# Strided masks of two batches on VectorE, fewer warm-up products, and expert weights loaded later and from ScalarE

## The chip, the core and the metric

The kernel runs on one core of one Trainium2 chip. The metric is the device time of one execution in microseconds (us). TensorE is written PE in profiles, VectorE DVE, ScalarE ACT, GpSimd POOL, and SyncE SP.

## What is computed

An attention block of 8 batches, 8 heads, 576 tokens and head size 64 is followed by a mixture of 8 experts. Heads 0 to 3 see the last 32 tokens; heads 4 to 7 see the earlier tokens of their own residue class modulo 32.

```python
mask_local = (rel >= 0) & (rel < stride)
mask_strided = (rel >= 0) & (pos[None, :] % stride == pos[:, None] % stride)
scores = np.where(masks[None, :, :, :], scores, -1000000000.0)
attn = softmax(scores);  x = attn @ v
...
e = fresh_e if s == 0 or local_gate[b, s] < 0.5 else prev_e
h = np.maximum(x[b, s] @ w1[e], 0.0)
out[b, s] = p[e] * (h @ w2[e])
```

Each token goes through one expert: the one its own logits choose, or the one of the token before it, as a gate says.

## The kernel before

**Attention.** `attention` walks over 32 head pairs, four to a batch: pairs 0 and 1 are local, 2 and 3 strided. One iteration n issues the load of pair n + 4 (`load`, L169 for q and k, L173 for values), the scores of pair n in two units (`scores`), the transposes of pair n - 2 (`turn_x`, L330), and the values and the normalization of pair n - 1 (`values` L288, `norm` L301 and L302). Router work, logits (L354) and gates (L382) come in fixed iterations, and two lists, `also` and `steps`, hang further work on them. There are five q/k buffers, two score banks in PSUM and two value banks, so a load waits until the scores of the pair five before it are done.

A local unit's mask is a multiplication by 0 and 1 on VectorE after the exponential (`mask`, L275). A strided unit's mask is a product ahead of its scores: an identity times `maskS`, with large negative numbers at the hidden places (L258), into the same bank, onto which the score products (L264) add. `maskS` is built at the start from two index tables.

At the very start `busy(WARM)` issues ten products of zeros (L184), 512 columns each. Products by twos are how f32 shows in the records.

**SyncE's order.** All q, k and value loads are issued by SyncE in the order of the program, and so are the stores of attention's rows to DRAM from batch 1 on (`store_x`): two DMAs for a local half (L314), ten for a strided half (L320). Expert 0's weights come in eight pieces of 512 KB (L724 for w1, L727 for w2), one an iteration from n = 5 to 12, after the load of that iteration. From n = 10, two of the sixteen weight sums of expert 0 (`sums`, L732) run on VectorE at each iteration's end.

**Experts.** `Experts.run` multiplies pairs of row tiles (128 rows each) by an expert's weights with seven products for eight (Strassen-like; `pair_hidden` L835, `pair_output` L871), which needs the sums and differences of weight blocks that `sums` makes. Two weight buffers `W` alternate: while expert e runs, the weights of e + 1 are loaded and summed. For each expert the first pair of tiles runs, then a second (`rest`), and then a `tc.Switch` of seven arms takes the remaining tiles: more pairs, a single tile (L926, L937) or half a tile (L947, L967). `pair_hidden` and `pair_output` call `run(steps)` at nine places, four and five; the lists of lists that `slots` builds say how many pending steps run at each place. Rows are gathered (L765) and scattered (L791) by GpSimd.

The weights of experts 1 to 7 are two SyncE DMAs of 2 MB each, issued as soon as their buffer is free; SyncE is no part of the switch, so it may issue while an arm still runs.

Of the kernel before, what the change touches and what calls it, by code (L numbers as in the profile page):

```python
# [8 lines left out]
F32 = mybir.dt.float32  # L9
# [3 lines left out]
Alu = mybir.AluOpType  # L13
# [5 lines left out]
P = 128  # L19
B, H, S, DH = 8, 8, 576, 64  # L20
# [19 lines left out]
GK, GL = PL * GC, PL * GR  # L40
# [15 lines left out]

TRUST = 1e12

WARM = 10

FILL = 4

TWINS = {b: b - 1 for b in range(1, B - 1, 2) if b % RB}

# [83 lines left out]
def attention(ctx, tc, qkl, qks, vl, vs, wg, xd, ident, router, moe):  # L148

    nc = tc.nc  # L150
    sums, probs, codes = router.sums, router.probs, router.codes
    consts = ctx.enter_context(tc.tile_pool(name="consts", bufs=1))
# [32 lines left out]

    busy(WARM)

# [21 lines left out]
    maskS = consts.tile([GK, 2 * GK + GL], BF16, name="maskS")  # L209
# [3 lines left out]
    for n, c in blocks:  # L213

        i, div = consts.tile([GK, 1], I32, name=f"row{n}"), consts.tile([GK, 1], F32, name=f"div{n}")
# [7 lines left out]
    n = GK  # L223
    nc.vector.tensor_copy(maskS[:, 0:2 * n].rearrange("p (a x) -> p a x", a=2), across(apart[n], [n, 2, n]))
    nc.vector.tensor_copy(maskS[:, 2 * n:], apart[GL])
    fold = consts.tile([P, 32], F32, name="fold")
    ci = consts.tile([P, E], I32, name="ci")
    down = consts.tile([P, E], F32, name="down")
    pi = consts.tile([P, CH], I32, name="pi")
    pos8 = consts.tile([P, CH], F32, name="pos8")  # L230
    start = consts.tile([P, CH], F32, name="start")

    def more_constants():

# [15 lines left out]
    def scores(u):  # L250
        t = st["qk", u.b, u.pair]
        kb, width = (LK, LQ) if u.local else (GK, GK)
        ps = psS.tile([P, 2, 512], F32, name="sps")
        sp = spans(u)
        n = sp[-1][2] + sp[-1][1]
        if not u.local:
            for h in range(2):
                nc.tensor.matmul(ps[0:GK, h, 0:n], lhsT=identb[0:GK, 0:GK],  # L258
                                 rhs=maskS[:, 0:n], start=True, stop=False, skip_group_check=True)
        for j, w, c in sp:  # L260
            m = kb if u.local else w
            for h in range(2):
                r = slice(h * DH, (h + 1) * DH)
                nc.tensor.matmul(ps[0:m, h, c:c + w], lhsT=t[r, S + j * width:S + j * width + m],  # L264
                                 rhs=t[r, j * width:j * width + w],
                                 start=(u.local and c == 0), stop=True, skip_group_check=True)
        e = work.tile([P, 2, 2 * GK + GL], F32, name="e")
        nc.scalar.activation(e[0:kb, :, 0:n], ps[0:kb, :, 0:n], Act.Exp, bias=0.0, scale=1.0 / DH ** 0.5)  # L268
        u.e = e

    def mask(u):
        if u.local:
            ev = u.e[:, :, 0:3 * LQ]
            m = maskL[:, 3 * u.g:3 * u.g + 3].rearrange("p a x -> p (a x)")
            nc.vector.tensor_tensor(ev, ev, m.rearrange("p (o x) -> p o x", o=1).to_broadcast([LK, 2, 3 * LQ]),  # L275
                                    op=Alu.mult)

    def values(u):
# [151 lines left out]
        u.n = n  # L430

    also = {n: [] for n in range(len(units) + 3)}
    also[1] = [more_constants]
    also[2] = [router.constants]
    n = PAIRS * RB + 3
# [4 lines left out]
    m = n  # L440
    rooms = (moe.spot[0].rearrange("p a x -> p (a x)")[:, 0:1024], moe.spot[1].rearrange("p a k x -> p (a k x)"),
             moe.spot[2].rearrange("p i a x -> p (i a x)"))
    early = router.table(0, bank, rooms)
# [5 lines left out]
    steps = []  # L449
    for n in range(len(units) + 3):  # L450
        if n < len(units):
            if n + ahead < len(order):
                load(*order[n + ahead])
            if 5 <= n < 13:
                moe.W[0].load(nc, moe.w1, moe.w2, 0, n - 5)
            if n == 10:
                steps = moe.W[0].sums(nc.vector)
            for u in units[n]:
                scores(u)
                mask(u)  # L460
        if 0 <= n - 2 < len(units) and order[n - 2][1] % 2 == 1:
            store_x(units[n - 2][1])
        if 0 <= n - 2 < len(units) and n != len(units):
            turn_x(*order[n - 2])
        if 0 <= n - 1 < len(units):
            for u in units[n - 1]:
                values(u)
                norm(u)
        if n == len(units):
            turn_x(*order[n - 2])  # L470
            moe.turn(moe.first, spare, 0)
        elif n == len(units) + 1:
            busy(FILL)
        for b in range(B):
            last = PAIRS * b + PAIRS - 1
            if n == last + 3 and b + 1 not in TWINS:
                gates(b)
            if n == last + 4 and b < B - 1 and b + 1 not in TWINS:
                for both in {TWINS.get(b, b), b}:
                    store_p(both)  # L480
            if n == last + 2:
                logits(b)
        for do in steps[:2]:
            do()
            steps.remove(do)
        if n == len(units) + 1:
            moe.turn(moe.first, bank, 1)
            busy(2)
            moe.row_sums(moe.first)
        for do in also[n]:  # L490
            do()
# [215 lines left out]
class Weights:  # L707
# [11 lines left out]
    def load(self, nc, w1, w2, e, piece=None):  # L719

        w1, w2 = w1[e].rearrange("(k p) f -> p k f", p=P), w2[e].rearrange("(k p) f -> p k f", p=P)
        if piece is None or piece < DK:
            c = slice(0, DK) if piece is None else slice(piece, piece + 1)
            nc.sync.dma_start(out=self.w1[:, c], in_=w1[:, c])  # L724
        if piece is None or piece >= DK:
            c = slice(0, FK) if piece is None else slice(2 * (piece - DK), 2 * (piece - DK) + 2)
            nc.sync.dma_start(out=self.w2[:, c], in_=w2[:, c])  # L727

    def sums(self, engine):

# [25 lines left out]
class Experts:  # L756
# [40 lines left out]
    def run(self, ctx):  # L797
        nc, tc, w1, w2, router = self.nc, self.tc, self.w1, self.w2, self.router
# [3 lines left out]
        W = self.W  # L802
# [176 lines left out]
        def load(e, w):  # L979
            w.load(nc, w1, w2, e)  # L980
            return w.sums(nc.vector)

        def slots(todo, counts):

            return [[todo.pop(0) for _ in range(min(n, len(todo)))] for n in counts]
# [13 lines left out]
        def rest(e, w, spot, pair, steps, nxt, index=None):  # L999

            self.gather(nxt)
            if index is None:
                steps = [[lambda: chosen.append(choose(e))]] + steps
            part1, part2 = pair_output(pair, w, pair_hidden(pair, w, steps))
            part1(steps)
            index = index or chosen.pop()
            flip = state["flip"]

            for arm in tc.Switch(index, ARMS, hint=f"expert{e}"):
                state["flip"] = flip  # L1010
                left = list(steps)
                more = []
                if arm > 3:
                    more.append(rows(spot, e, (4, 5)))
                if arm % 4 > 1:
                    more.append(rows(spot, e, (4 + arm // 4 * 2,)))
                if arm % 2:
                    more.append(rows(spot, e, (4 + arm // 2,), HALF))
                if more:
                    self.gather(more[0])  # L1020
                part2(more[0] if more else nxt, left)
                for i, r in enumerate(more):
                    then = more[i + 1] if i + 1 < len(more) else nxt
                    if i + 1 < len(more):
                        self.gather(then)
                    if r.m < P:
                        half(r, w, then, left)
                    elif r.n == 1:
                        single(r, w, then, left)
                    else:  # L1030
                        output(r, w, pair_hidden(r, w, left), then, left)
                while left:
                    run(left)
# [4 lines left out]
        sums = load(1, W[1])  # L1038
# [11 lines left out]
        second = rows(0, 1, (2, 3))  # L1050
# [6 lines left out]
        h = pair_hidden(other, W[1], places)  # L1057
# [1 line left out]
        nxt = rows(1, 0, (2, 3))  # L1059
        rest(1, W[1], 0, second, [[lambda: next(arms)] for _ in range(4)], nxt)  # L1060
        second = nxt
        sums = load(2, W[1])
        nxt = rows(0, 2, (0, 1))
        rest(0, W[0], 1, second, slots(sums, [0, 1, 2, 1, 2, 2, 2, 2]) + [[f] for f in sums], nxt)
        for e in range(2, E - 1):
            w, first = W[(e + 1) % 2], nxt
            second = rows(1, e, (2, 3))
            self.gather(second)
            steps = slots(load(e + 1, W[e % 2]), [0] * 5 + [1, 1, 1, 3] + [1] * 8 + [2])
            nxt = rows(0, e + 1, (0, 1))  # L1070
            h = pair_hidden(first, w, steps)
            index = choose(e)
            output(first, w, h, second, steps)
            rest(e, w, 1, second, steps, nxt, index)
# [473 lines left out]
```

## Time and profile before

| | us |
|---|---|
| median of 3 runs | 677.26 (677.22 to 678.85) |
| the profiled execution's own time | 677.25 |
| its span | 675.5 |
| TensorE busy (modelled) | 661.2 |
| VectorE busy | 353.9 |
| ScalarE busy | 195.4 |
| attention, until the first expert product | 158.4 |

The span is what the profile covers; the 1.75 us around it belong to the execution too. A TensorE that waits inside its pipeline counts as busy, so its share is an upper bound. The chain of waits follows, from the last instruction backwards, what each one waited for last. The timeline of SyncE shows how long each DMA took to issue, which includes waiting for a place; when a DMA has landed is read from the semaphore updates that the trace records.

### The profile page before, as it was taken

How to read it: one execution, taken by the hardware profiler on the slowest of the kernel's cores; microseconds unless marked ns; L12 is line 12 of the kernel's file. 1: busy time of each engine (PE TensorE's matmuls, PEld its weight loads, DVE VectorE, ACT ScalarE, POOL GpSimd, SP SyncE). 2: the span in 40 equal slices, each digit the busy share in tenths (PEclk: the TensorE clock that was granted, in tenths of full speed). 3: DMA queues.
4: the chain of work that ended last, by engine and by line, in shares of the span. 5: the costliest groups of instructions: out<-in, count | busy, mean ns of one | idle time of the engine just before them, and what ended most of it. 6: DMA issues, size and time to landing. Idle time of an engine off the chain costs nothing.

```text
span 675.5 us, 14755 instructions
## 1 busy us (share of the span) xinstructions
PE 661.2 (98%) x6019; PEld 569.9 (84%) x6020; DVE 353.9 (52%) x783; ACT 195.4 (29%) x364; POOL 109.3 (16%) x132
## 2 busy tenths in 40 slices
PE   9999999999999999999999999999999999999995
PEld 6888888888999999599979999996799899699594
DVE  5658876956884447126523664651256546522122
ACT  3545445453312221321222222121222132221320
POOL 3401010122022023012011202302011112121001
PEclk9999999999999999999999999999999999999999
DMA  9998787875311081171145217101712622011001
GB/s 324 391 353 276 267 282 258 280 239 195 124 65 49 18 312 58 28 283 49 36 155 172 65 52 265 64 21 40 262 41 65 220 93 73 34 43 58 17 9 37
DMA packets 36435, 95.85 MB, mean 142 GB/s; under 512 B 4594, under 2 KB 12658, under 8 KB 36262
## 3 DMA queue, kind: packets, MB, share of 16 engines
q1 hardware_dynamic: 28438, 72.59, 30.7%
q0 software_dynamic: 7296, 21.19, 9.8%
q8 instruction: 67, 1.10, 0.7%
q14 instruction: 106, 0.87, 0.4%
q10 hardware_dynamic: 528, 0.10, 0.1%
HBM read 74.69 MB, written 19.69 MB: 140 GB/s over the span
## 4 chain that ended last, share of the span: by engine, by line
PE 94%; DVE 2%; DMA 1%; issue 1%; ACT 0%; SPq 0%; POOL 0%; DVEq 0%; POOLq 0%; ACTq 0%
PE lps L835 30%; PE mps L871 29%; PE sps L264 6%; PE vps L288 6%; PE lps L926 4%; PE mps L937 4%; PE tps L330 3%; PE xps L778 2%; PE mps L967 2%; PE lps L947 2%; PE sps L258 2%; DMA qk<-in_qks_dram 1%; PE tps L354 1%; PE vps L184 1%; PE tps L382 1%
## 5 line engine op out<-in xcount | busy, mean ns | idle before, releaser
L791 POOL DMA_INDIRECT out_dram<-y,tab x40 | 45.8, 1146 | 351.0 <-DVE y L823 246.6
L835 PE MATMUL lps<-tt,ws 128*128 128x128 f32 x768 | 91.5, 275 | 0.0
L835 PEld LDWEIGHTS lps<-tt,ws 128*128 128x128 f32 x768 | 88.5, 192 | 0.2
L871 PE MATMUL mps<-wt,k 128*128 128x256 f32 x384 | 85.7, 380 | 0.0
L871 PEld LDWEIGHTS mps<-wt,k 128*128 128x128 f32 x384 | 72.8, 190 | 9.9
L835 PE MATMUL lps<-xt,w1t 128*128 128x128 f32 x512 | 63.1, 276 | 3.0 <-ACT y L973 1.9
L835 PEld LDWEIGHTS lps<-xt,w1t 128*128 128x128 f32 x512 | 60.4, 192 | 6.5 <-ACT y L973 3.7
L823 DVE TENSOR_TENSOR h<-lps,u 128x512 f32<-128x512 f32 x48 | 33.2, 691 | 58.6 <-PE lps L835 58.5
L871 PE MATMUL mps<-w2t,h 128*128 128x256 f32 x256 | 60.5, 379 | 0.0
L268 ACT ACTIVATE e<-sps 128x576 f32<-128x576 f32 (+1 forms) x64 | 41.7, 651 | 54.7 <-PE sps L264 53.5
L765 POOL DMA_INDIRECT x<-xd,gi x40 | 40.2, 1005 | 82.4 <-PE lps L835 24.0
L871 PEld LDWEIGHTS mps<-w2t,h 128*128 128x128 f32 x256 | 47.4, 190 | 5.8
L264 PE MATMUL sps<-qk 64*128 64x96 f32 (+2 forms) x704 | 50.9, 282 | 0.8 <-DMA qk<-in_qks_dram 0.8
L822 ACT ACTIVATE h<-h 128x512 f32<-128x512 f32 x48 | 30.2, 630 | 70.1 <-DVE h L823 69.0
L264 PEld LDWEIGHTS sps<-qk 64*128 64x128 f32 (+2 forms) x704 | 42.9, 185 | 9.0 <-issue 6.5
L822 ACT ACTIVATE h<-lps 128x512 f32<-128x512 f32 (+1 forms) x28 | 15.6, 563 | 81.8 <-PE lps L835 62.6
L823 DVE TENSOR_TENSOR u<-lps,p 128x512 f32<-128x512 f32 x16 | 11.1, 691 | 51.8 <-PE lps L835 31.4
L771 ACT ACTIVATE x<-x 128x512 f32<-128x512 f32 (+1 forms) x40 | 27.1, 717 | 32.7 <-DMA x<-xd,gi 21.3
L779 ACT COPY xt<-xps 128x512 f32<-128x512 f32 (+1 forms) x38 | 20.3, 565 | 51.4 <-PE xps L778 51.4
L835 PE MATMUL lps<-xt,ws 128*128 128x128 f32 x256 | 31.3, 275 | 0.0
L835 PE MATMUL lps<-tt,w1t 128*128 128x128 f32 x256 | 31.3, 275 | 0.0
L871 PE MATMUL mps<-w2t,k 128*128 128x256 f32 x128 | 30.4, 380 | 0.0
(238 smaller groups left out, 952.2 us busy)
## 6 DMA issues: line engine op xcount, KB each, us to landing
w1t<-in_w_dram SPq DMA_DIRECT2D x7, 2048.0 KB
w2t<-in_w_dram SPq DMA_DIRECT2D x7, 2048.0 KB
qk<-in_qkl_dram SPq DMA_DIRECT2D x16, 592.0 KB
qk<-in_qks_dram SPq DMA_DIRECT2D x16, 576.0 KB
vl<-in_vf_dram SPq DMA_DIRECT2D x8, 780.0 KB
vs<-in_vg_dram SPq DMA_DIRECT2D x8, 639.8 KB
xd<-xl SPq DMA_DIRECT2D x14, 288.0 KB
xd<-xs SPq DMA_DIRECT2D x56, 63.0 KB
```

The costliest lines, as they stand in the source:

```text
L264: nc.tensor.matmul(ps[0:m, h, c:c + w], lhsT=t[r, S + j * width:S + j * width + m], rhs=t[r, j * width:j * width + w], start=(u.local and ...
L268: nc.scalar.activation(e[0:kb, :, 0:n], ps[0:kb, :, 0:n], Act.Exp, bias=0.0, scale=1.0 / DH ** 0.5)
L288: nc.tensor.matmul(ps[a * HALF:(a + 1) * HALF, h, i], lhsT=u.e[0:m, h, q0:q0 + HALF], rhs=vt[0:m, j, 2 * i2 + h], start=(i == 0 and h == 0 ...
L765: self.nc.gpsimd.indirect_dma_start(out=r.x[0:r.m, i], out_offset=None, in_=self.xd[0:r.rows], in_offset=bass.IndirectOffsetOnAxis(ap=r.gi ...
L771: self.nc.scalar.activation(r.x[0:r.m, i, 0:D], r.x[0:r.m, i, 0:D], Act.Copy, scale=r.gate[i][0:r.m])
L791: s = self.nc.gpsimd.indirect_dma_start(out=self.out, out_offset=bass.IndirectOffsetOnAxis(ap=r.si[i][0:r.m], axis=0), in_=y[0:r.m, i], in ...
L822: relu = lambda o, i: nc.scalar.activation(o, i, Act.Relu)
L823: add = lambda o, i, p: nc.vector.tensor_tensor(o, p, i, op=Alu.add)
L835: nc.tensor.matmul(ps[:, f], lhsT=m[:, kk, f * P:(f + 1) * P], rhs=v[:, kk], start=(start and f == 0 and kk == 0), stop=(kk == 1), skip_gr ...
L871: nc.tensor.matmul(ps[:, 0:256], lhsT=m[:, f], rhs=v[:, f], start=(start and f == 0), stop=(f == 3), skip_group_check=True)
L926: nc.tensor.matmul(ps[:, f], lhsT=w.w1[:, kk, c:c + P], rhs=r.xt[:, 0, kk], start=(f == 0 and kk == 0), stop=(kk == DK - 1), skip_group_ch ...
L937: nc.tensor.matmul(ps, lhsT=h[f // 4][:, f % 4], rhs=w.w2[:, f], start=(f == 0), stop=(f == FK - 1))
```

## The change

- Ten warm-up products become eight.
- For batches 0 and 1 (`MB = 2`), strided units have no mask product. Their score products start their bank, and VectorE multiplies the exponentials by `near`, a 0/1 version of `maskS` that is made at the end of iteration 0. Their last block computes 126 rows of which 72 are used. For that the host puts k ahead of q in the strided array, so that the extra columns read are q's.
- Expert 0's pieces are loaded in iterations 8 to 15 (5 to 12 before), and its sums start in iteration 13 (10 before).
- The weights of experts 2 to 7 are issued by ScalarE in four DMAs of 1 MB. They are steps now: for expert 2 at places 1, 1, 2 and 3 of expert 0's second pair (place 0 is the switch's choice), for the others at places 0 to 3 of the next expert's first pair, after the switch's exit. The sums are spread anew over the places behind them.

```diff
-WARM = 10
+WARM = 8
+MB = 2
...
+    near = consts.tile([GK, 2 * GK + GL], F32, name="near")
+    def masks():
+        nc.vector.tensor_scalar(near, maskS, 0.0, None, Alu.is_equal)
...
-        if not u.local:
+        early = u.b < MB
+        if not u.local and not early:
             for h in range(2):
                 nc.tensor.matmul(ps[0:GK, h, 0:n], lhsT=identb[0:GK, 0:GK],
                                  rhs=maskS[:, 0:n], start=True, stop=False, skip_group_check=True)
         for j, w, c in sp:
-            m = kb if u.local else w
+            m = kb if u.local or early else w
             for h in range(2):
                 r = slice(h * DH, (h + 1) * DH)
-                nc.tensor.matmul(ps[0:m, h, c:c + w], lhsT=t[r, S + j * width:S + j * width + m],
-                                 rhs=t[r, j * width:j * width + w],
-                                 start=(u.local and c == 0), stop=True, skip_group_check=True)
+                k0, q0 = (S, 0) if u.local else (0, S)
+                nc.tensor.matmul(ps[0:m, h, c:c + w], lhsT=t[r, k0 + j * width:k0 + j * width + m],
+                                 rhs=t[r, q0 + j * width:q0 + j * width + w],
+                                 start=((u.local or early) and c == 0), stop=True, skip_group_check=True)
...
+        elif u.b < MB:
+            n = 2 * GK + (GL if u.g else 0)
+            ev = u.e[0:GK, :, 0:n]
+            nc.vector.tensor_tensor(ev, ev, near[:, 0:n].rearrange("p (o x) -> p o x", o=1).to_broadcast([GK, 2, n]),
+                                    op=Alu.mult)
...
+    also[0] = [masks]
...
-            if 5 <= n < 13:
-                moe.W[0].load(nc, moe.w1, moe.w2, 0, n - 5)
-            if n == 10:
+            if 8 <= n < 16:
+                moe.W[0].load(nc, moe.w1, moe.w2, 0, n - 8)
+            if n == 13:
                 steps = moe.W[0].sums(nc.vector)
...
+    def quarters(self, q, w1, w2, e):
+        w1, w2 = w1[e].rearrange("(k p) f -> p k f", p=P), w2[e].rearrange("(k p) f -> p k f", p=P)
+        def step(o, x, c):
+            return lambda: q.dma_start(out=o[:, c], in_=x[:, c])
+        return [step(self.w1, w1, slice(2, 4)), step(self.w1, w1, slice(0, 2)),
+                step(self.w2, w2, slice(0, 4)), step(self.w2, w2, slice(4, 8))]
...
-        sums = load(2, W[1])
+        loads, sums = W[1].quarters(nc.scalar, w1, w2, 2), W[1].sums(nc.vector)
         nxt = rows(0, 2, (0, 1))
-        rest(0, W[0], 1, second, slots(sums, [0, 1, 2, 1, 2, 2, 2, 2]) + [[f] for f in sums], nxt)
+        rest(0, W[0], 1, second, slots(loads, [2, 1, 1]) + slots(sums, [0, 0, 1, 1, 2, 2, 2, 2]) + [[f] for f in sums], nxt)
...
-            steps = slots(load(e + 1, W[e % 2]), [0] * 5 + [1, 1, 1, 3] + [1] * 8 + [2])
+            v = W[e % 2]
+            steps = slots(v.quarters(nc.scalar, w1, w2, e + 1), [1] * 4)
+            steps += slots(v.sums(nc.vector), [0, 0, 1, 1, 2, 2] + [1] * 6 + [2, 2])
...
-    qks = np.concatenate([heads(classes(i["q"][:, h2:])), heads(classes(i["k"][:, h2:]))], 3)
+    qks = np.concatenate([heads(classes(i["k"][:, h2:])), heads(classes(i["q"][:, h2:]))], 3)
```

## The prediction

> **What bounds the kernel now.** I read the page first, then the chain of work that ended last, by windows, then SyncE's own timeline. The page shows TensorE busy for 98% of the span, and DMA full only in the first quarter:
>
> ```profile
> PE 661.2 (98%) x6019; PEld 569.9 (84%) x6020; DVE 353.9 (52%) x783; ACT 195.4 (29%) x364; POOL 109.3 (16%) x132
> DMA  9998787875311081171145217101712622011001
> ```
>
> A modelled busy share says little, so I went through the chain. From 1.4 to 94 us and from 158 us to the end it is TensorE almost throughout. Its start, with the pieces that the change takes out:
>
> ```profile
> 1.36 4.45 PE vps L184 x10
> 5.81 3.95 PE sps L264 x48
> 9.76 1.55 PE vps L288 x48
> 11.31 0.36 PE sps L258 x2
> 11.67 0.64 PE sps L264 x8
> 12.30 0.42 PE sps L258 x2
> ```
>
> L258 is the mask product; one strided pair has 0.36 + 0.42 = 0.78 us of it. In attention's second half the chain leaves TensorE:
>
> ```profile
> 94.24 1.34 PE vps L288 x40
> 95.58 0.38 SPq L169
> ...
> 96.02 1.75 SPq L173
> ...
> 97.86 8.40 DMA qk<-in_qks_dram
> ...
> 106.31 0.71 PE sps L264 x8
> ```
>
> The scores of pair 23 (n counts head pairs, four to a batch) wait for a q/k load that SyncE issued at 97.86, though the program puts it at n = 19, which TensorE ran at 87. SyncE is ten microseconds behind, and its timeline says why:
>
> ```profile
> 77.44 0.39 SPq L169 DMA_DIRECT2D qk<-in_qks_dram  x1
> ...
> 82.27 13.19 SPq L320 DMA_DIRECT2D xd<-xs  x10
> 95.56 0.40 SPq L169 DMA_DIRECT2D qk<-in_qks_dram  x1
> 96.02 1.75 SPq L173 DMA_DIRECT2D vs<-in_vg_dram  x1
> 97.86 0.34 SPq L169 DMA_DIRECT2D qk<-in_qks_dram  x1
> ```
>
> Ten stores of 63 KB take 13.2 us to issue. In the trace's semaphore records SyncE's DMAs go round eight semaphores and each waits until the one eight before it has landed, so the stores come out only as the loads ahead of them land. I call four pairs' loads with their twelve stores a **round**. Rounds begin at 55.11 (n = 10), 77.44, 95.56, 115.13 and 133.09, back to back. **Two clocks** thus run side by side, TensorE and the ring, and at 106 us the ring is the later one, by 0.85 us (gap in TensorE's starts at 105.25).
>
> **What the Trainium skill says.** "DMA: Bandwidth & Descriptors", section on issuing engines that are not separate DMA queues: DMAs of all engines end on the same 16 engines, so another issuer saves only issue time. The trace agrees in what it shows: 2 MB of weights issued at 401.43, with nothing ahead, landed at 410.98, and issuing took 0.37 us. "Runtime: NRT & Kernel Launch", section Instruction fetch mechanics: a taken branch out of the fetched pages waits for a DMA. GpSimd stands 5.3 to 6.4 us after six switch exits with weights in flight, 2.6 and 3.3 after the two without. TensorE does not: from its last start in an arm to its next it takes 0.84 us with weights in flight (at 480.4) and without (592.7 and 642.3). "TensorE: Matmul & The Clock Gate", section What's actually happening: the clock rises only after a full activity window. Score products come in twos that start 207 ns apart until about 7.4 us and 105 ns apart later, as it says.
>
> **The change, part by part.**
> *Warm-up.* Two products fewer at 0.43 us (4.45/10) = 0.86 us. Pair 0's q/k landed at 4.71, before the eighth ends at 4.9, so the scores start then; but at half clock until 7.4. 12 pairs of products at 0.207 from 4.9 end at 7.4, against 7.83 now: 0.43 gained. Bounds 0.4 and 0.9; taken 0.45.
> *Masks off TensorE.* Two batches, two strided pairs each: 4 x 0.78 = 3.1 us. By n = 8, at 37 us, TensorE is 3.6 us early. Loads of pairs 2 and 3 landed at 10.42 and 14.30 and would now be wanted at 10.8 and 14.5: just in time.
> *Masks on VectorE.* Eight multiplies of 126x504 or 126x648, f32. The local mask of the same kind shows the price:
>
> ```profile
> L275 DVE TENSOR_TENSOR e<-e,maskL 128x576 f32<-128x576 f32 x32 | 23.0, 754 | 9.1 <-ACT e L268 8.9
> ```
>
> Scaled by elements 0.66 and 0.85, so 6.0 us in the first 35, where VectorE is 2 to 4 us of every 5 busy. A pair's values come one iteration later, over 3 us of TensorE work; VectorE's constants at n = 2 (16.6 to 19.0) are the one crowd, and leave about 0.8. Taken at nothing; without that cover up to 1 us once. The 0/1 mask itself is one operation of 0.3 to 0.5 us in idle time. The wider last block (126 weight columns for 72) hides under the streams. Exchanging q and k in the array costs nothing.
> *Expert 0's weights three iterations later.* This decides. They are eight SyncE DMAs of 512 KB. The queue is full from 2 to 50 us and lands in order, 1.25 to 1.5 us for a piece: the three of n = 5 to 7 landed 1.53, 1.26 and 1.25 after the ones ahead. Gone from there, round n = 10 can begin 4.0 us earlier, at 51.1; TensorE, 3.6 early, lets the loads go as early. But that round now has four pieces for three, and round n = 14 two for none. A round with three took 77.44 - 55.11 = 22.3, one with none 95.56 - 77.44 = 18.1: 1.4 a piece; by landings 1.25. So +1.3 and +2.8, and round n = 18 begins at 95.56 - 4.0 + 1.3 + 2.8 = 95.6, **where it began before**. Pair 22 lands 4.2 later (99.8); TensorE needs 4.75 from there to pair 23 (100.71 to 105.45 now), so 104.6. Pair 23 landed 10.7 after its round began here, but 9.2 and 9.1 in the rounds before and after: this one has the 1.75 us issue above, where others take 0.41. I know no cause that the change keeps or removes, so I take the middle, 9.7: it lands at 105.3, for 106.26. **Gain 1.0**, bounds 0 and 1.75; the other 2.6 of TensorE's early gain end as waits at n = 18 to 23. Next come pair 26 (landed 119.25, wanted 120.23) and VectorE's stretch of 111 to 122, which starts from pair 24's scores: both follow a gain of this size.
> *Expert 0's sums later.* Sixteen VectorE adds of 0.68, two an iteration, move from n = 10..17 to 13..20.
>
> ```profile
> 82.00:96.00 14.00, 14.00 (x240) 11.89 (x240) 9.73 (x32) 6.80 (x13) 2.64 (x4) 1.00 0.86 288
> ```
>
> VectorE has 9.73 busy of these 14 us (third column); 4.1 more fill it. The second add wants piece 3, landing near 62 to 63, when VectorE comes to it near 60; masks and norms queue behind. Both delays fall where TensorE is ahead of the ring. Taken at nothing; at most 1 us, if backlog reaches 111.
> *Weights on ScalarE.* Two issues leave SyncE for each of experts 2 to 7, where by then nothing stands behind them; four go onto ScalarE after the copy of the first product and the first relus. Bounds for one: 0.37 (weights on SyncE) and 2.07 (its slowest at 99.30). ScalarE stands idle 3.9, 1.9 and 1.2 us there, so 0.4 each is covered; queued behind are the relus of h22 and h21, for which VectorE's k sums and TensorE's output products wait, with about 2 us in hand. The first 2 MB must land before the sums of slot 6: issued 3.6 and 8 us after the exit, 9.5 us to land, so by 18; slot 6 is at 21. Slot 16 has two sums for one, ahead of the row sums: 0.2 to 0.35 at the two exits (405.7, 532.5) where TensorE waits for VectorE's last adds. Gathers start some 3 us earlier, but ScalarE's scaling at 424.6 already finds them landed (420.8). **Cost 0.3**, bounds 0 and 0.6.
>
> Sum: -1.0 + 0.3 = -0.7. The profiled execution took 677.25 (span 675.5 and 1.75 outside), the median is 677.26. **Forecast 676.5**, own range 675.4 to 677.8.
>
> **Rivals.**
> *The whole gain arrives.* If pieces in the rounds cost nothing, falling into the stretches in which stores leave DMA 0.2 to 0.4 full (74 to 78), round n = 18 begins near 91.5 and pair 23 is no longer late. Then 3.55 and part of the 0.85 stall go: 677.25 - 4.0 + 0.3 = 673.5, with bounds 672.8 and 674.2. For it: a fifth of a round has idle DMA. Against: the stores there wait for the last load's landing, and the 22.3 against 18.1.
> *The early relief is not handed on.* If round n = 10 begins by the stores' own norms or by TensorE's releases and not by the queue, only the +4.1 in rounds n = 10 and 14 counts: pair 23 lands at 106.3 + 4.1 - 1.0, and the kernel ends at 677.25 + 3.1 + 0.3 = 680.6. It decides below 1.4 us of relief, where the loss passes 0.3%. Against: the flights of 10 to 12 us until 42.
> *ScalarE's issues block.* At 1.4 to 2.1 us each, as SyncE's slow ones, two in a row overrun the 2 us in hand by 1, six experts: 677.25 - 1.0 + 6 = 682. Against: 0.37 for all of SyncE's later weights.
>
> **Chances.** Forecast 0.50, whole gain 0.35, no relief 0.10, blocked issues 0.05. A measurement of this kernel tells 0.3%, 2 us, from no change: faster 0.35, same 0.50, slower 0.15. The range reaches into the second case and stops short of the last two: 673.0 to 678.4.
>
> **What would show it.** L258 has 48 products for 64; the chain still passes through a q/k load near n = 22 or 23, with round n = 18 beginning at 95 to 96.5. If it begins before 93, the pieces were free; after 97, the relief was lost. ScalarE's weight issues stay under 0.5 us and TensorE's gaps at exits at 0.84 to 0.94.

## The result, and the profile after

The change is slower: 682.1 us (median of 11 executions, 680.1 to 686.0) against 678.84 for the kernel before on the same chip, ratio 1.0071 [1.0052, 1.009] (the 95% interval, here and below). The changed kernel run once more gave 681.66 against 678.41, 1.003 [1.0004, 1.0056]. I had forecast 676.5, 0.7 below a median of 677.26; the 678.84 has those three executions and eight more.

The profiled execution took 685.56 us (span 683.8), 8.3 more than that of before, while the medians differ by 3.3. So this profile shows more than the usual loss, and I use a second one beside it (span 682.1). I say that an engine *stands* while it starts nothing, though work is next in its program. The page's lines that answer those of before, with the queue that brings TensorE's code:

```profile
PE 660.3 (97%) x6002; PEld 569.9 (83%) x6002; DVE 359.4 (53%) x792; ACT 195.5 (29%) x364; POOL 110.0 (16%) x132
...
DMA  9989777874511116135205315411262262011001
...
q8 instruction: 68, 1.11, 0.7%
```

TensorE's busy time is about the same (660.3, 661.2 before), though it has less to do, and the span is 8.3 longer: TensorE stands. The chain of waits at the place that I had shown of before:

```profile
78.18 10.81 DMA qk<-in_qks_dram
...
89.04 0.71 PE sps L273 x8
...
91.70 1.47 PE tps L344 x6
...
98.64 0.87 PE sps L273 x12
...
99.52 5.92 DMA qk<-in_qks_dram
...
105.48 0.71 PE sps L273 x8
```

Before, one q/k load of this stretch was late, by 0.85 us. Now two are, by 2.37 (pair 19) and 1.69 us (pair 22). SyncE's timeline (start, how long the issue took, line) shows the round that sets the second:

```profile
76.00 0.65 SPq L171 DMA_DIRECT2D qk<-in_qks_dram  x1
...
87.63 11.78 SPq L334 DMA_DIRECT2D xd<-xs  x10
99.52 0.40 SPq L171 DMA_DIRECT2D qk<-in_qks_dram  x1
```

Round n = 14 begins at 76.0 (77.44 before) and n = 18 at 99.5 (95.56 before; I had 95.6). The windows behind the first wait (window, its length, then busy time of PE, PEld, DVE, ACT and POOL, then the granted clock, DMA share, GB/s) show something that no part of my sum had:

```profile
86.00:89.90 3.90, 1.60 (x18) 1.15 (x17) 2.94 (x13) 0.38 (x2) 0.61 (x1) 1.00 1.05 378
89.90:93.30 3.40, 3.40 (x24) 2.60 (x24) 0.69 (x1) 1.29 (x3) 2.03 (x4) 0.50 1.04 422
93.30:99.00 5.70, 5.70 (x122) 5.07 (x120) 4.71 (x12) 3.20 (x7) 0.00 (x0) 1.00 0.47 147
```

For 3.4 us behind the wait TensorE runs at **half clock** (0.50 granted): the six transposes of this stretch, in the chain above, take 1.47 us, and 0.81 at full clock before. The same follows the second wait. The wait costs its own length and about 1.5 us more.

Where the time went, from the first score product of each pair in both traces: 3.8 us early at n = 8 (3.6 forecast); 1.4 lost at n = 9 and 1.6 at n = 14 in stands; 2.4 at n = 19 and 1.5 behind it at half clock; 1.7 at n = 22 and 0.7 behind it (half clock again, less the 0.85 that the kernel before waits there). The first expert product starts at 163.8 (158.35 before), 5.5 late, and the experts take 520.0 us in place of 517.2. The stand at n = 9 lies inside a value product's run, in the chain:

```profile
35.80 0.84 PE vps L302 x22
36.65 1.11 issue
37.76 0.74 PE vps L302 x17
```

No buffer and no data is waited for ("issue"). The DMA records show one packet of 16 KB on q8, TensorE's code, from 35.03 to 36.23; TensorE goes on 1.5 us after its end. The stand that begins at 59.4 lies behind a packet that ends at 59.43, and TensorE goes on 1.5 us after that end too. "Runtime: NRT & Kernel Launch", section Instruction fetch mechanics, says that code is fetched in blocks of 256 instructions while the block before runs, mostly hidden. The trace agrees: its packets have 16 KB, and up to the experts one comes for every 251 TensorE instructions in the mean (253 before). These stands are where it was not hidden.

### The profile page after: what moved, and what is told of

It is laid out like the page before. It is cut to its first block, busy times and chain, and to the rows that moved or that the text cites. A ratio compares the mean times of both kernels' runs of the same rounds, so it can differ in the third digit from the quotient of the medians.

```text
span 683.8 us, 14746 instructions
## 1 busy us (share of the span) xinstructions
PE 660.3 (97%) x6002; PEld 569.9 (83%) x6002; DVE 359.4 (53%) x792; ACT 195.5 (29%) x364; POOL 110.0 (16%) x132
## 4 chain that ended last, share of the span: by engine, by line
PE 89%; DMA 4%; DVE 2%; issue 2%; ACT 1%; SPq 1%; POOL 0%; DVEq 0%; POOLq 0%; ACTq 0%
PE lps L858 30%; PE mps L894 27%; PE vps L302 5%; PE sps L273 5%; PE lps L949 4%; PE mps L960 4%; DMA qk<-in_qks_dram 4%; PE tps L344 3%; PE xps L801 2%; PE mps L990 2%; PE lps L970 2%; PE sps L265 1%; PE tps L368 1%; PE tps L396 1%; PE lps L980 0%
## 5 line engine op out<-in xcount | busy, mean ns | idle before, releaser
L273 PE MATMUL sps<-qk 64*128 64x96 f32 (+3 forms) x704 | 50.0, 282 | 4.8 <-DMA qk<-in_qks_dram 4.5
L802 ACT COPY xt<-xps 128x512 f32<-128x512 f32 (+1 forms) x38 | 20.3, 565 | 50.7 <-PE xps L801 50.7
```

The costliest lines, as they stand in the source:

```text
L273: nc.tensor.matmul(ps[0:m, h, c:c + w], lhsT=t[r, k0 + j * width:k0 + j * width + m], rhs=t[r, q0 + j * width:q0 + j * width + w], start=( ...
```

## The experiments

My theory after the result had two parts. **The code's place:** taking 36 instructions out of TensorE's stream (33 with three added waits) moves the experts' code against the packets it comes in, so that TensorE stands behind exits. **The ring:** q/k loads, weights and stores take the masks' gain in attention, as forecast, and long waits also halve the clock. "The experts" below is the time from the first expert product to the end of the profile. Rivals: VectorE's masks, ScalarE's issues, or the later weights cause the loss directly. Ratios are to the kernel before on the same chip.

*The parts one by one*: each is the change reduced to the part named.

**Masks and shorter warm-up alone.**

```diff
-WARM = 10
+WARM = 8
+MB = 2
```

> The kernel before with the masks and the warm-up of the change alone (weights as before). Ring theory: TensorE is some 3.5 us early by pair 8, but pairs 18 to 23 wait for SyncE's ring, whose bytes have not moved, so pair 23 starts where it did: 0 to 1 us faster in all. Rival, masks make VectorE late: 2 us or more slower. Rival, TensorE decides: 3.5 us faster.

Measured: 684.16, 1.0087 [1.0055, 1.0119]. Attention ends 1.1 early, but the experts take 525.5 us in place of 517.2. That is slower than the whole change, and lies where the masks do nothing.

**Later weights of expert 0 alone.**

```diff
-            if 5 <= n < 13:
+            if 8 <= n < 16:
...
-            if n == 10:
+            if n == 13:
```

> The kernel before with expert 0's eight pieces and sums three iterations later, and nothing else. Ring theory: the round from n = 14 gets two pieces where it had none and starts its successor 3 to 5 us later, while the relief ahead is cut short because TensorE is not early; pairs 22 and 23 wait, 3 to 5 us slower. Rival, the loss lies elsewhere (scattered stalls for instructions, the experts): within 1 us of before.

Measured: 678.16, 1.0015 [0.9994, 1.0036]. The round of n = 10 begins at 50.75 (55.11 before) and that of n = 18 at 96.3 (95.56): what leaves the early round is paid back by n = 18, at no gain and little loss. A loss of 3 us from the ring alone, one of the readings, is not there.

**ScalarE's issues alone.**

```diff
-            steps = slots(load(e + 1, W[e % 2]), [0] * 5 + [1, 1, 1, 3] + [1] * 8 + [2])
+            steps = slots(v.quarters(nc.scalar, w1, w2, e + 1), [1] * 4)
+            steps += slots(v.sums(nc.vector), [0, 0, 1, 1, 2, 2] + [1] * 6 + [2, 2])
```

and the like for expert 2.

> The kernel before with the weights of experts 2 to 7 issued by ScalarE in four parts and the new places of the sums, and nothing else. If the loss seen between 231 and 273 us in the changed kernel's profile belongs to it: 1.5 to 3 us slower, with ScalarE and VectorE standing at the entry of expert 0's arm while the weights fly, attention unchanged. Rival, that loss was chance or comes from attention: within 0.7 us of before.

Measured: 680.36, 1.0032 [1.002, 1.0044]; experts 520.4. All 24 issues take 0.37 to 0.90 us, so they do not block.

**The change without ScalarE's issues**, the first two edits together.

> The changed kernel with the weights of experts 2 to 7 back on SyncE (masks, warm-up and the later weights of expert 0 kept). Ring theory: the loss of attention stays: 2 to 5 us slower than before, pair 23 starting at 109 to 112. Rival, ScalarE's issues make the loss: within 1 us of before or faster.

Measured: 686.37, 1.0132 [1.0097, 1.0168]; pair 23 at 106.1 and not at 109 to 112, so I missed attention; the loss is 6.5 us of experts (523.7). Round n = 18 begins at 95.4. ScalarE's issues are thus no loss on top of the masks: with them the loss is 3.3 us and not 8.2.

*The place of the code.* The chain of the masks-only kernel behind expert 1's exit:

```profile
239.63 1.80 PE lps L850 x16
241.43 2.87 issue
244.30 1.86 PE lps L850 x7
```

After sixteen products TensorE stands, and 0.8 us before it goes on the clock halves until 250.3 (seven products in 1.86 us). Product by product against the kernel before, 1.1 us are lost behind the branch into the first switch, 5.9 at this point and 1.3 behind expert 0's exit. If the place is the cause, putting the count of instructions back must heal it, and moving the unchanged kernel's code must break it.

**Filled up at the start** (added to the masks alone).

> The masks and the shorter warm-up alone, with TensorE's instruction count restored: six warm-up products and eighteen products of 2x2, so that the experts' code begins 5277 TensorE instructions into the program, against 5278 before and 5245 with the masks alone. Theory of the code's place: TensorE's code comes in single 16 KB packets of 256 instructions, and the masks moved the exits of the experts against these packets. Then the stands at 241 us (3.05 us) and 297 us (1.25 us) and the half-clock window behind them are gone, the experts take the 517 us of before, and the kernel ends 0.5 to 1.5 us below before. Rival, VectorE's masks or the ring cause it: the stands stay, 684.

```diff
-WARM = 8
+WARM = 6
+TINY = 18
+    for _ in range(TINY):
+        nc.tensor.matmul(ps[0:2, 0:2], lhsT=warm[:, 0:2], rhs=warm[:, 0:2], start=True, stop=True)
     busy(WARM)
```

Measured: 679.26, 1.0017 [1.0006, 1.0027], so some 5 us better than without, but not below before. The stands are gone and the experts take 517.1. The gain in attention was lost to the padding itself: the clock is full only from 14.2 us (7.4 before). The same chain, now without a stand:

```profile
239.34 1.73 PE mps L891 x8
241.07 5.02 PE lps L855 x45
```

**The kernel before, moved.**

> The kernel before with two warm-up products and 119 products of 2x2 in place of ten warm-up products: nothing else is changed, but the experts' code begins 222 instructions later, the same place within 256 as with the masks alone. The start may be up to 3 us later. Theory of the code's place: from the first expert product to the end takes 522 to 526 us (517.1 before), with stands of TensorE of 1 to 3 us near the exits of experts 0 and 1. Rival, the masks themselves cause them: 517.

```diff
-WARM = 10
+WARM = 2
+TINY = 119
...
+        nc.tensor.matmul(ps[0:2, 0:2], lhsT=warm[:, 0:2], rhs=warm[:, 0:2], start=True, stop=True)
```

Measured: 690.21, 1.0176 [1.0147, 1.0205]. The first expert product is 2.9 us later, from the padding and two waits for loads; the experts take 528.4, more than I expected. Same exit, same point:

```profile
243.47 1.80 PE lps L840 x16
245.27 3.42 issue
248.68 1.45 PE lps L840 x7
```

No mask, weight or issue is changed here. Both kernels with code at this place also stand at the first switch's branch: in the trace TensorE's branch takes 3.41 us with the masks alone and 3.29 us here, and 0.45 us in the filled-up kernel. No weights are in flight there (DMA share 0.00 and 0.02 around it with the masks alone), so at this branch the place alone decides.

**Filled up at attention's end.**

> The masks and the shorter warm-up alone, with sixteen products of 2x2 ahead of the filler products at attention's end, so that the experts' code begins 5277 TensorE instructions into the program (5278 before, 5245 with the masks alone) and attention is that of the masks alone. Theory of the code's place: the first expert product about 1 us earlier than before, as with the masks alone, no stand of TensorE at the exits at 241 and 297 us, experts 517 us: 0.5 to 1.5 us below before. Rival, the first padding helped by slowing attention and not by the place: the stands are back and the kernel ends at 682 to 684.

```diff
+TINY = 16
...
+            for _ in range(TINY):
+                nc.tensor.matmul(ps[0:2, 0:2], lhsT=warm[:, 0:2], rhs=warm[:, 0:2], start=True, stop=True)
             busy(FILL)
```

The warm-up keeps its eight. Measured: 678.83, 1.0015 [1.0, 1.0031]. Experts 518.0, so the place is confirmed and the rival falls; but the 1.5 us that pair 28 is early go, and 1.4 more: in a stand of 0.7 us at 142.3 behind a packet, in a half-clock window from 145.7, and in the sixteen products. I had expected below before; it isn't.

**Without weights in flight** (the masks alone; experts 2 to 7 then compute with the weights of experts 0 and 1).

> The masks and the shorter warm-up alone, without padding; the loads of the weights of experts 2 to 7 are left out, so that these experts compute with the weights of experts 0 and 1. If a stand at an exit needs both the code's place and weights in flight: TensorE's next page is fetched about 1 us after each exit, in place of 3.7 to 5.4, the stands at 241 and 297 us and the half clock are gone, and the experts take 517 to 519 us: 677 to 679. If the place alone makes them: 684.

```diff
         def load(e, w):
-            w.load(nc, w1, w2, e)
+            if e < 2:
+                w.load(nc, w1, w2, e)
```

Measured: 679.68, 1.0041 [1.0023, 1.0059], experts 520.4, between the two readings. The chain at the same point:

```profile
240.21 2.04 PE lps L850 x16
242.25 0.95 issue
243.20 2.83 PE lps L850 x23
```

The stand at 297 and the half clock are gone, and this one shrinks from 2.87 to 0.95. The trace gives a reason. With SyncE's weights in flight, TensorE's next packet starts 3.7 to 5.4 us after the start of an exit's branch; with none, 0.9 to 2.5 us. So at exits the code's place decides whether TensorE gets to the packet's end first, and the weights decide how late the packet is. Of the 3.2 us that are still lost, 1.0 is lost at the first switch's branch, which takes 3.35 us here too, and 2.0 at expert 1's exit: weights make the stand longer, and it does not need them.

*ScalarE's issues again.* They start behind the exit, so the packet comes early there (1.0 to 2.7 us in the change), which would be why they help the moved code. But they are in flight when expert 0's arm is entered. The chain of the change:

```profile
262.80 0.69 DVE k L908
263.49 4.59 issue
268.08 0.04 DVEq L1032
```

VectorE stands 4.6 us behind its own branch (the next 8 KB packet of code in the records ends at 266.5), and TensorE loses 0.9 us to it. With ScalarE's issues alone TensorE loses 1.5 us in this arm, and 1.6 more late in the kernel:

```profile
571.36 5.18 PE mps L879 x24
576.54 1.35 issue
577.89 4.12 PE mps L879 x18
```

There TensorE's branch into a switch takes 3.66 us (0.33 before), with no weights in flight (DMA share 0.00 in the 4 us ahead of it). ScalarE's issues also add waits to TensorE's stream, twelve in this trace, so that this may be the code's place again; no run tests it.

**ScalarE's issues without expert 2's.**

```diff
-        loads, sums = W[1].quarters(nc.scalar, w1, w2, 2), W[1].sums(nc.vector)
+        sums = load(2, W[1])
```

> The kernel before with ScalarE's four issues for experts 3 to 7 alone; expert 2's weights are issued by SyncE as before. If ScalarE's late weights for expert 2 delay the fetch behind the branch into expert 0's arm: that fetch comes 1.1 us after the branch at 254 us again (5.3 with all of them), the stand of 1.3 us at 259 us is gone, and the kernel is 1 to 1.5 us below the version with all of ScalarE's issues (680.4), near before plus 1. Rival, the stand there is chance: no difference.

Measured: 678.14, 1.0006 [0.9993, 1.0019]. The stand is gone, the experts take 517.3, and TensorE's packet comes 1.1 us after the branch. The theory holds for expert 0's arm. The stand at 576 is gone too (that branch takes 0.33 us), which the theory had not said.

*Attention.* **The change without the later weights.**

> The change without the later weights of expert 0. If the later weights cost attention its gain: the first expert product comes about 1 us before that of before (157.3) and the experts take 2 to 3 us more, as in the change: 679. If attention's loss comes from the masks and TensorE's fetches: the first expert product stays 3 us or more behind, 682.

Measured: 680.81, 1.0055 [1.0032, 1.0077]; experts 519.6. The first expert product at 159.1 lies between the two readings: pair 18's load is late by 1.8 us, and a half-clock window follows. So it tells nothing about the weights.

**The whole change, filled up.**

> The whole change with TensorE's instruction count restored as in the first of these kernels. Theory of the code's place: stands of TensorE behind its own packets in attention (1.3 and 1.5 us at 36 and 59) and the one at 267 us move or go, the waits for q/k loads at n = 19 and 22 stay: 679 to 681.5. Rival, the ring and ScalarE's issues are all of it: 682.

As the first padding. Measured: 681.1, 1.0046 [1.0026, 1.0066]. Attention ends 0.3 early, round n = 18 begins at 97.0; the experts still take 520.1, with the stand in expert 0's arm and one at 577 behind a branch of 3.78 us. That is what ScalarE's issues alone cost at the old place (520.4). So in the whole change the two causes do not add up: putting the count back takes nothing certain off its loss.

**The change again.**

> The changed kernel again, unchanged, for a second profile. If attention's loss in the first profile (5.5 us at pair 23) was made of stands behind TensorE's own packets and of half-clock windows that not every execution meets: the first expert product comes 158 to 161.5 here (163.8 in the first), and the experts lose 2 to 3 us as in the first. If the loss belongs to the code: stands at 36 and 59 us again and 163 to 164.

The stands at 36 and 59 us are absent: they belonged to one execution. Round n = 18 begins at 96.25. Pair 18's load is late by 1.4 us and pair 22's by 3.2 us, at 99; these and a half-clock window behind the second put pair 23 2.3 us late. The experts take 521.5, more than the 2 to 3 us of loss that I had expected.

**Weights after the ring.** This kernel and the next three have the masks, SyncE's weights for experts 1 to 7, and, except where it is said, the sixteen products at attention's end.

> As the one before, with expert 0's eight pieces of weights loaded two at a time at n = 27 to 30, after the last q/k load, and the sums from n = 30 on. If the ring takes the masks' gain and the pieces are what it carries: the scores of pair 27 start 3.5 to 5 us before those of before (126.3), in place of about 1; the end then loses up to 4 us again to sums that come late. If stores and loads alone set the ring: pair 27 at 125 or later.

```diff
-            if 5 <= n < 13:
-                moe.W[0].load(nc, moe.w1, moe.w2, 0, n - 5)
-            if n == 10:
+            if 27 <= n < 31:
+                for i in range(2):
+                    moe.W[0].load(nc, moe.w1, moe.w2, 0, 2 * (n - 27) + i)
+            if n == 30:
...
-        for do in steps[:2]:
+        for do in steps[:4]:
```

Measured: 677.79, 1.0004 [0.999, 1.0018]. Round n = 18 begins at 84.5, no load is late, and pairs 23 to 28 are 3.6 us early. With the weights at n = 5 to 12 the same masks were 3.5 early at n = 14 and 0.6 at n = 18, and round n = 18 began at 94.9: eight pieces make 10.4 us of it, 1.3 each (1.25 to 1.4 in my sum). So the ring does take the masks' gain, and the pieces are what it carries. Here late weights and sums take it back at the end: the chain waits until 146.4 for a w2 piece, then for VectorE's sums and norms.

**Weights at n = 21 to 28.**

> The masks and the shorter warm-up alone, with sixteen products of 2x2 ahead of the filler products at attention's end, and expert 0's pieces loaded at n = 21 to 28 with the sums from n = 26, two an iteration. If the pieces in the ring are what took the masks' gain, and the code's place what made the experts slow: pair 27 at 122.5 to 123.5 (126.3 before), the first expert product at 154.5 to 156, the experts 517 us: 673 to 675. Rival, late sums or VectorE take the gain at attention's end, as with the weights at n = 27 to 30: 677 to 678.

```diff
-            if 27 <= n < 31:
-                for i in range(2):
-                    moe.W[0].load(nc, moe.w1, moe.w2, 0, 2 * (n - 27) + i)
-            if n == 30:
+            if 21 <= n < 29:
+                moe.W[0].load(nc, moe.w1, moe.w2, 0, n - 21)
+            if n == 26:
...
-        for do in steps[:4]:
+        for do in steps[:2]:
```

Measured: 678.96, 1.001 [0.9996, 1.0024]: the rival. Pair 28 is 3.7 early, then VectorE is full from 126 to 136 (9.86 of 10 us) with the router's table and the sums (`ws`), and TensorE waits 2.3 us for the rows that it transposes:

```profile
130.46 0.60 DVE xt L665
...
133.70 0.56 DVE xs L318
134.25 1.20 DVE ws L752 x2
135.45 0.20 DVE got L678
...
135.69 0.77 PE tps L346 x5
```

A half-clock window follows that wait too.

**The same without the sixteen products.**

> The one before without its sixteen small products, so that the experts' code begins at 5245 again. Theory of the code's place: attention as in the one before, but the experts take 6 to 8 us more, with stands at the exits of experts 1 and 0: 679 to 682. Rival, the stands belonged to the weights' timing in attention: as the one before.

Measured: 684.88, 1.008 [1.0052, 1.0107]; attention as before it, experts 524.4 in place of 517.2. The place of the code, a third time.

**Weights in two halves** (with the sixteen products).

> As with expert 0's pieces at n = 21 to 28 and sixteen small products at attention's end, but the four w1 pieces at n = 14 to 17 with their sums at n = 20 to 23, and the four w2 pieces at n = 24 to 27 with their sums from n = 30: no sums in VectorE's full stretch from 111 to 136 us, where the kernel with pieces at n = 21 to 28 stood 2.5 us. If ring, VectorE's stretch and code's place are all that took the masks' gain: pair 28 about 3.5 us before that of before, the first expert product at 154.5 to 156, the experts 517 us: 673 to 675.5. Rival, the end of attention is bound by the router on VectorE: first expert product at 157 or later, 676.5 or more.

```diff
-            if 21 <= n < 29:
-                moe.W[0].load(nc, moe.w1, moe.w2, 0, n - 21)
-            if n == 26:
+            if 14 <= n < 18 or 24 <= n < 28:
+                moe.W[0].load(nc, moe.w1, moe.w2, 0, n - (14 if n < 18 else 20))
+            if n == 20:
...
-        for do in steps[:2]:
+        for do in steps[:2] if n < 24 or n > 29 else []:
```

Measured: 677.69, 0.9991 [0.9976, 1.0005]. The profiled execution took 674.42: first expert product at 155.4 (2.9 early), experts 517.2, no stand over 1.1 us. But it is the fastest of 22, and I had forecast such times for the median.

**The two-halves kernel and the kernel before once more.**

> The kernel with expert 0's weights in two halves (w1 at n = 14 to 17, w2 at n = 24 to 27) once more, for a second profile and interval. Its executions lay between 674.4 and 680.3, the profiled one at 674.42, the fastest. If the further limit that most of them meet shows in a profile: the first expert product comes 1.5 to 4 us later than 155.4, behind a stand with a half-clock window or one behind TensorE's own packets, the experts still 517: 676 to 678.5. If nothing differs: 674 to 675 and the first expert product at 155.4.

> The kernel before once more, for a second profile: how far two executions of the same kernel lie apart, and where. If before has no stand that depends on the execution: the first expert product within 0.5 us of 158.35, the experts 517. Else stands of 1 to 1.5 us behind TensorE's own packets or q/k loads move it by up to 3 us.

Measured: 676.72 against 679.17, 0.997 [0.9956, 0.9984], its profile 675.03; again the fastest execution, so what slows the others stays open. This version beats the change clearly. Against the kernel before it is 0.16 to 0.44% faster in this measurement, and not told from it in the other. The kernel before gave 678.48 against the same 679.17, 0.9991 [0.9975, 1.0008], a span of 675.4 (675.5 in its first profile) and the same experts. Its attention is up to 1.2 us earlier on the way; its clock was full from 4.7 us and not from 7.4.

All profiles by the place of the experts' code (TensorE instructions ahead of it, to within three; 255 more is nearly the same place in packets of 256) and by who issues the weights of experts 2 to 7:

| place | weights | experts, us |
|---|---|---|
| 5278, as before | SyncE | 517.2, 517.2 (before); 517.1, 517.2, 517.2, 517.4, 517.5, 518.0, 518.2 |
| the same | ScalarE, experts 3 to 7 | 517.3 |
| the same | ScalarE, all | 520.1, 520.4 |
| 5245, or 5500 (the last) | SyncE | 523.7, 524.4, 525.5, 528.4 |
| 5245 | ScalarE, all | 519.6; 520.0, 521.5 (the change) |
| 5245 | none | 520.4 |

## Why the prediction was wrong

**The step that failed** is the sentence on TensorE at the exits: it "does not" stand there, with weights in flight or without. I read it off three exits of one program, in one measure, the time from the last product of an arm to the next, and let it stand for the changed program. It was true of the code's place, not of branches. The measure was blind too: in the first profile of the change it still reads 0.84 us at four exits, and 1.00 at the two with the added sum. The stands lie elsewhere behind the branches. Product by product against the kernel before, the experts of the two profiles lose 1.3 and 1.1 us behind the branch into the first switch, 0.3 and 1.7 at expert 1's exit and the sixteen products behind it, and 1.0 and 1.4 in expert 0's arm. In my sum the experts had only +0.3, for ScalarE's issues; they measured +2.8 and +4.3.

Cutting 36 instructions was costed as time saved and never as code moved. With SyncE's weights, the moved code costs 6.5 to 8.3 us with the masks, and 11.2 in the kernel before. ScalarE's later weights give about half of that back or more. They have a price of their own, 3 us at the old place of the code: 1.2 to 1.5 in expert 0's arm, and 1.6 or 1.7 behind the late branch, whose cause is not shown. How the loss of the whole change divides between the two edits therefore stays open: it is 2.4 to 4.3 us with the code moved, and 3 us without. The difference of the medians, 3.3 us, is about what the experts lost; how attention stood in the executions without a profile isn't known.

**Attention** was forecast at -1.0 and measured +5.5 and +2.3. Point by point:

- *Warm-up.* Scores start at 4.8 (I had 4.9). Pair 2 is 1.6 us early in place of 0.45, but in the second profile of before it is 1.2 early too, with ten products: most of that gain is the clock's, not the change's. I had taken the end of the half clock, 7.4, as fixed; it was 4.55 in the changed kernel's profile.
- *Masks off TensorE.* 48 mask products are left, and n = 8 is 3.8 us early (3.6). The agreement is luck: pair 1 was 1.5 early already, the scores of a strided pair took 1.25 to 1.32 us in place of 2.19 (some 0.9 saved four times, 0.78 priced), and 1.3 us went in four short waits that I had put at nothing, 0.56 of it for pair 3's load, which I had called just in time. Against the second profile of before n = 8 is only 2.6 early. The scores of pairs 3 and 7:

```profile
14.27 1.32 PE sps L273 x20
...
30.22 1.25 PE sps L273 x20
```

- *Masks on VectorE.* Eight multiplies at 0.66 and 0.84 us, nearly all hidden, as taken.

```profile
L289 DVE TENSOR_TENSOR e<-e,near x8: 660/748/835, 11.6 to 32.3; 126x504 f32<-126x504 f32 x4, 126x648 f32<-126x648 f32 x4
```

- *The ring.* Round n = 10 begins at 50.7 (51.1). Round n = 18 was to begin where it began before, 95.6: it does at 95.4, 96.3, 96.25 and 97.0 in four kernels or profiles with this order, and at 99.5 in the first profile. There round n = 14 took 23.5 us, against 20.7 in the second profile and 20.9 in my sum; why isn't known. The mechanism was right, and the runs with moved weights show it from the other side.
- *What a wait costs.* My sum priced the remaining waits at their length. Waits of 1.9 us and more between TensorE's starts brought half clock each time, 1.5 us more. With them, with the two stands for code in the first profile (3.0 us), and with one load later than its round explains (3.2 us in the second profile), the -1.0 is gone. That load, pair 22's, took 5.9 and 6.1 us from issue to landing in the two profiles, where I had kept the 4.2 of before. Why it took longer was not settled.
- *Sums later.* No cost is seen. *ScalarE's issues* took 0.37 to 0.64 us, 0.42 in the mean (0.4 taken), and the two exits with the added sum lost 0.06 us each (0.2 to 0.35 forecast). The cost of these issues was not on ScalarE: in expert 0's arm it was code that came late behind a branch.

Of the rivals, none named the code. The one that gave 682, blocked issues, met the time by chance: its mechanism did not occur. Of the signs that I named, the gaps at exits came out nearly as forecast and showed nothing of the loss. Round n = 18 at 99.5 in the first profile lies outside the signs (95 to 96.5), and one issue of 0.64 us is over the 0.5.

## What to carry to other kernels

An edit that takes instructions out ahead of a long, branching part moves that part's code against the packets it is fetched in. Before a change is judged by such a part, fill it up to the old count, or compare the part alone, product by product, in both traces: a gap measured at one chosen point misses a stand that comes sixteen products later. A large transfer in flight at a taken branch made the code behind it later still, here on TensorE, VectorE and GpSimd; let it start where no branch follows soon. And a wait of TensorE of about 2 us should be priced at its length plus a half-clock window, here 1.5 us.

## What the runs showed of the hardware

- In the twenty profiles, all twelve gaps of 1.89 us or more between TensorE's starts (between 5 and 660 us) come with a half-clock window of 3.41 us (once of two), which begins up to 1.6 us behind the gap or in its last 0.8. None of the gaps of 1.16 to 1.79 us does. "TensorE: Matmul & The Clock Gate", section Why this matters for your kernels, warns of gaps over about 3 us; here shorter ones were enough.
- What lies behind that border can be read off the clock records. In each trace every change of the clock lies on one grid of 3.41 us (in the changed kernel's profile the stretches of 85.33 and 13.65 us are 25 and 4 steps). Summed over the steps of the grid, TensorE's idle time (by modelled ends) was 1.6 us or more in the steps just before those twelve windows, and at most 1.4 in all others. So what counted was the idle time within one step, not the length of a gap: of the gap of 3.38 us at 99 in the changed kernel's second profile, 1.85 us fell into the step that halved the clock. One window, in the kernel filled up at attention's end, is an exception: it follows a step with only 0.5 us of idle time, and stays unexplained.
- TensorE goes on about 1.2 to 1.7 us after the end of the packet that it stands for (36.23 to 37.76 in the change; 242.76 to 244.30 and 296.96 to 298.43 with the masks alone).
- The next packet of TensorE's code starts 0.9 to 2.7 us after the start of a taken branch with no weights in flight, and 3.5 to 6.0 us with an expert's weights in flight.
